# A list scheduler sets the order of all instructions, and matmuls on a zero tile fill TensorE's waits before the first feed-forward

## The chip, the cores and the metric

One core of a Trainium2 chip. The metric is the device time of one execution in microseconds (us), the median of the runs taken; a single core has no second core to compare its clock with, so a run is called slow only where it is over 1.5% above the fastest run of the same kernel. "Span" is the length of one profiled execution; it lies 1.7 us below the time of that same run.

## The reference, cut to what matters

```python
# r, k, v: [4, 8, 768, 48] (batch B, heads H, sequence S, head size D)
for t in range(S):                                    # linear attention with a decaying state
    cur = einsum('bhd,bhe->bhde', u * k_t, v_t)
    y[:, :, t] = einsum('bhd,bhde->bhe', r_t, state + cur)
    state = w * state + einsum('bhd,bhe->bhde', k_t, v_t)
x = y.transpose(0, 2, 1, 3).reshape(4, 768, 384)
X = fft(fft(x, axis=1), axis=2)                       # Fourier mixing
u = x + real(X)
un = (u - mean) / sqrt(var + 1e-6)                    # over the 384 columns
return u + relu(un @ w_ch1) @ w_ch2                   # 384 -> 1536 -> 384
```

Each batch passes through four stages: attention, the Fourier transform (two matmul steps), normalising, and the feed-forward. The Fourier transform of a batch needs all of its attention; the feed-forward of one half of a batch (384 rows) needs that half's normalised rows.

## The kernel before

The sequence is cut into 24 chunks of 128 rows, six to a batch. `phase1` multiplies k and r of a chunk by a decay table (VectorE, tile `KR`), turns the product with eight TensorE transposes (`tp`) and copies it to `KRT` (ScalarE). `phase2` makes the scores `A_ps`, masks them (`MA`) and updates the state; `phase3` makes the outputs `yd_ps` and `X`. After a batch's sixth chunk come the first Fourier step (matmuls from `XF`, copies `TT`), the second (matmuls from `TT` and its reversed copy `TR`, six additions `UF`), the statistics, and the normalised rows `UN`, which must be transposed (`UNT`) before the feed-forward. The order is that of a hand-written loop, which the framework's own scheduler refines; all loads and the DMA transposes of `UN` share the queue of SyncE and keep program order.

```python
    def phase1(i):
        ...
        nc.vector.tensor_tensor(out=KR..., in0=kr..., in1=wtab..., op=AluOp.mult)
        V = wp.tile([128, H, D], BF16, name="V", bufs=4)
        cv = nc.scalar.copy(V, vt)
        if i == 0:
            tc.keep_in_program_order(cv)
        tp = ps.tile([128, 2, NP, 128], BF16, name="tp", bufs=1)
        for s in range(2):
            for p in range(NP):
                nc.tensor.transpose(tp[:, s, p, :], KR[:, s, p, :], ident)
        KRT = wp.tile([128, 2, NP, 128], BF16, name="KRT", bufs=4)
        nc.scalar.copy(KRT, tp)
    ...
            sp(nc.sync.dma_start_transpose(out=UNT.rearrange("p j c t -> p (j c) t"),
                                           in_=UN.rearrange("p j d -> p (j d)")))
    ...
    INP = 6                                   # chunks of input held at once
    for i in range(INP):
        load(i)
    load_tables()
    FG = None                                 # the Fourier transform under way
    MSTART = 10
    for s in range(NC + 2):
        if s < NC:
            phase1(s)
        if INP <= s + INP - 2 < NC:
            load(s + INP - 2)
        if FG:
            FG = FG if advance(FG, 3 if s < 12 else 1) else None
        if s >= MSTART:
            feed(2)                           # up to two pieces of feed-forward work
        if 1 <= s < NC + 1:
            phase2(s - 1)
        ...
        if s >= 2:
            phase3(s - 2)
        ...
    feed(len(M))
```

Of the kernel before, what the change touches and what calls it, by code (L numbers as in the profile page):

```python
# [15 lines left out]
B = 4  # L16
# [44 lines left out]

@with_exitstack
def kernel(
# [31 lines left out]

    icol_i = cp.tile([128, 1], mybir.dt.int32, name="icol_i")
# [49 lines left out]
    def load_tables():  # L146
        sp(nc.sync.dma_start(out=te_t, in_=te_c.ap()))
        sp(nc.sync.dma_start(out=to_t, in_=to_c.ap()))
        sp(nc.sync.dma_start(out=hid_t, in_=hid_c.ap()))

    def load_w1():
        with tc.issue_after(marks[2].ins):
            for dt in range(3):
                nc.gpsimd.dma_start(out=W1[:, dt, :], in_=w1[dt * 128:(dt + 1) * 128, :])

    def load_w2():
        with tc.issue_after(marks[6].ins):
            for fg in range(3):
                nc.gpsimd.dma_start(out=W2[:, fg * 4:(fg + 1) * 4, :],
                                    in_=w2[fg * 512:(fg + 1) * 512, :].rearrange("(f p) d -> p f d", p=128))  # L160

    marks = {}

    def sp(ins):
        return tc.keep_in_program_order(ins)

    NC = B * NQ
    bat = [{} for _ in range(B)]
    chk = [{} for _ in range(NC)]

    def load(i):
        b, q = divmod(i, NQ)
        sl = slice(q * 128, (q + 1) * 128)
        kr = inp.tile([128, 2, H, D], F32, name="kr")
        vt = inp.tile([128, H, D], F32, name="vt")
        sp(nc.sync.dma_start(out=kr[:, 0], in_=k[b, :, sl, :].rearrange("h p d -> p h d")))  # L176
        sp(nc.sync.dma_start(out=kr[:, 1], in_=r[b, :, sl, :].rearrange("h p d -> p h d")))
        if i == 0:
            sp(nc.sync.dma_start(out=ident, in_=id_c.ap()))
        sp(nc.sync.dma_start(out=vt, in_=v[b, :, sl, :].rearrange("h p d -> p h d")))  # L180
        if i == 0:
            sp(nc.sync.dma_start(out=mtri, in_=mtri_c.ap()))
        chk[i]["in"] = (kr, vt)


    def phase1(i):
        c = chk[i]
        kr, vt = c["in"]
        KR = KRs[i % NB]
        nc.vector.tensor_tensor(  # L190
            out=KR.rearrange("t s p (a d) -> t (s p) a d", a=2)[:, :, :, 0:D],
            in0=kr.rearrange("t s (p a) d -> t (s p) a d", a=2),
            in1=wtab.rearrange("t s (p a d) -> t (s p) a d", a=2, d=D), op=AluOp.mult)
        V = wp.tile([128, H, D], BF16, name="V", bufs=4)
        cv = nc.scalar.copy(V, vt)  # L195
        if i == 0:
            tc.keep_in_program_order(cv)
        tp = ps.tile([128, 2, NP, 128], BF16, name="tp", bufs=1)
        for s in range(2):
            for p in range(NP):  # L200
                nc.tensor.transpose(tp[:, s, p, :], KR[:, s, p, :], ident)  # L201
        KRT = wp.tile([128, 2, NP, 128], BF16, name="KRT", bufs=4)
        nc.scalar.copy(KRT, tp)  # L203
        PR = wp.tile([128, NP, 128], BF16, name="PR", bufs=4)
        nc.vector.tensor_tensor(out=PR, in0=KRT[:, 0], in1=KRT[:, 1], op=AluOp.mult)  # L205
        c.update(KR=KR, V=V, KRT=KRT, PR=PR)

    def phase2(i):
        b, q = divmod(i, NQ)
        c = chk[i]  # L210
        KR, V, KRT = c["KR"], c["V"], c["KRT"]
        A_ps = [ps.tile([128, NP, 128], F32, name="A_ps", bufs=2) for _ in range(2)]
        for p in range(NP):
            for a in range(2):
                rows = slice(a * 64, a * 64 + 64)
                nc.tensor.matmul(A_ps[a][:, p, :], lhsT=KRT[rows, 0, p, :], rhs=KRT[rows, 1, p, :],  # L216
                                 start=(p == 0), stop=(p == NP - 1), skip_group_check=True)
        MAs = []
        for a in range(2):
            MA = wp.tile([128, NP, 128], BF16, name="MA", bufs=6)  # L220
            if a == 0 and b > 0:
                nc.vector.tensor_tensor(out=MA, in0=A_ps[a], in1=mtri.unsqueeze(1).to_broadcast([128, NP, 128]),
                                        op=AluOp.mult)
            else:
                AC = wp.tile([128, NP, 128], BF16, name="AC", bufs=2)
                nc.scalar.copy(AC, A_ps[a])  # L226
                nc.gpsimd.affine_select(out=MA, in_=AC, pattern=[[0, NP], [1, 128]], base=0,  # L227
                                        channel_multiplier=-1, compare_op=AluOp.is_gt, fill=0.0)
            MAs.append(MA)
        S = c.get("S")  # L230
        if q < NQ - 1:
            u_ps = ps.tile([128, NP, 2, D], F32, name="u_ps", bufs=1)
            for p in range(NP):
                nc.tensor.matmul(u_ps[:, p, :, :], lhsT=KR[:, 0, p, :], rhs=V[:, 2 * p:2 * p + 2, :],
                                 start=(p == 0), stop=(q == 0 and p == NP - 1), skip_group_check=True)
            if q > 0:
                nc.tensor.matmul(u_ps, lhsT=ident, rhs=S, start=False, stop=True, skip_group_check=True)
            Sn = wp.tile([128, NP, 2, D], BF16, name="Sst", bufs=4)
            nc.vector.tensor_tensor(out=Sn, in0=u_ps, in1=WD, op=AluOp.mult)
            chk[i + 1]["S"] = Sn  # L240
        c["MA"] = MAs

    def phase3(i):
        b, q = divmod(i, NQ)
        c = chk[i]
        V, KRT, PR, MAs, S = c["V"], c["KRT"], c["PR"], c["MA"], c.get("S")
        if q == 0:
            bat[b]["X"] = bp.tile([128, NQ, DM], BF16, name="X")
            bat[b]["EO"] = bp.tile([128, 2, 3, DM], BF16, name="EO", bufs=1)
            bat[b]["XF"] = bp.tile([128, 2, 3, DM], BF16, name="XF")  # L250
        X = bat[b]["X"]
        yd_ps = ps.tile([128, DM + H], F32, name="yd_ps", bufs=1)
        y_ps = yd_ps[:, 0:DM].rearrange("t (h d) -> t h d", h=H)
        for p in range(NP):
            nc.tensor.matmul(yd_ps[:, DM + 2 * p:DM + 2 * p + 2], lhsT=PR[:, p, :], rhs=UW[:, p, :],
                             start=(p == 0), stop=False, skip_group_check=True)
        if q > 0:
            for p in range(NP):
                nc.tensor.matmul(y_ps[:, 2 * p:2 * p + 2, :], lhsT=KRT[:, 1, p, :], rhs=S[:, p, :, :],
                                 start=False, stop=False, skip_group_check=True)  # L260
        DE = wp.tile([128, H], F32, name="DE")
        nc.scalar.copy(DE, yd_ps[:, DM:])  # L262
        TT = wp.tile([128, H, D], BF16, name="TT")
        marks[i] = nc.gpsimd.tensor_tensor(out=TT, in0=V, in1=DE.unsqueeze(2).to_broadcast([128, H, D]),  # L264
                                           op=AluOp.mult)
        for a in range(2):
            for p in range(NP):
                h = 2 * p + a
                nc.tensor.matmul(y_ps[:, h, :], lhsT=MAs[a][:, p, :], rhs=V[:, h, :],  # L269
                                 start=False, stop=(h == H - 1), skip_group_check=True)  # L270
        nc.vector.tensor_tensor(out=X[:, q, :], in0=yd_ps[:, 0:DM],  # L271
                                in1=TT.rearrange("p h d -> p (h d)"), op=AluOp.add)
        if b == 0 and q >= 3:
            fold(b, q - 3, q - 2)
        elif q == NQ - 1:
            fold(b, 0, 3)

    def fold(b, n0, n1):
        X, EO, XF = bat[b]["X"], bat[b]["EO"], bat[b]["XF"]
        lo, hi = X[:, n0:n1, :], X[:, n0 + 3:n1 + 3, :]  # L280
        nc.vector.tensor_tensor(out=EO[:, 0, n0:n1, :], in0=lo, in1=hi, op=AluOp.add)
        nc.vector.tensor_tensor(out=EO[:, 1, n0:n1, :], in0=lo, in1=hi, op=AluOp.subtract)
        e, o = EO[:, :, n0:n1, 0:192], EO[:, :, n0:n1, 192:384]
        nc.vector.tensor_tensor(out=XF[:, :, n0:n1, 0:192], in0=e, in1=o, op=AluOp.add)
        nc.vector.tensor_tensor(out=XF[:, :, n0:n1, 192:384], in0=e, in1=o, op=AluOp.subtract)


    def fourier(b):
        X, XF = bat[b]["X"], bat[b]["XF"]
        TT = bp.tile([128, 3, 2, 386], BF16, name="TT2")  # L290
        TR = bp.tile([128, 3, 2, 384], BF16, name="TR", bufs=1)
        for cb in range(3):
            for par in range(2):
# [163 lines left out]
```

## Time and profile before

| | before |
|---|---|
| time, median of 3 (lowest to highest) | 235.19 us (232.9 to 235.21) |
| span of the profile | 233.5 us |
| first feed-forward matmul starts | 63.7 us |
| from there to the end of the last matmul | 164.6 us |
| from there to the end of the span | 5.2 us |

The last three rows add up to the span (63.7 + 164.6 + 5.2 = 233.5). The first is a stretch in which loads, VectorE, ScalarE and TensorE hand work to one another and no engine is full. The second is a stretch in which TensorE has all of the feed-forward to do; what it takes above the warm duration of that work is idle time and half clock. The prediction below shows the lines.

### The profile page before, as it was taken

The page shows a single profiled execution, that of the slowest core. Times are in us where ns is not written, and L with a number is a line of the kernel's source. Part 1 is how long each engine was busy: PE and PEld are TensorE (multiplying, and loading weights), DVE is VectorE, ACT ScalarE, POOL GpSimd, SP SyncE. Part 2 cuts the span into 40 slices and gives each one's busy share as a digit, 9 for nine tenths or more (in the row PEclk, how much of TensorE's full clock was granted, in tenths as well). Part 3 has the DMA queues.
Part 4 walks back from the last instruction along what each step waited for, and adds up shares of the span by engine and source line. Part 5 has one row for each costly group of instructions (what it writes and reads, how often), then busy time and mean ns, then how long its engine had stood idle before and what let it go on. Part 6 is the DMA issues. An engine that isn't in the chain of part 4 may idle for free.

```text
span 233.5 us, 4269 instructions
## 1 busy us (share of the span) xinstructions
PE 191.2 (82%) x1640; PEld 122.3 (52%) x1640; DVE 131.1 (56%) x273; ACT 129.3 (55%) x261; POOL 64.1 (27%) x93
## 2 busy tenths in 40 slices
PE   0289856991798979987999789964999999999990
PEld 0156634670555645665565456652565565566660
DVE  4367479795955694598881454782841277101020
ACT  4677534734798675577247564543356637654500
POOL 4038944701213441343100133162001000101021
PEclk9999999999599988995599999995699999999998
DMA  5999999999999996101603940102003103310111
GB/s 108 187 188 197 284 206 186 181 190 190 175 177 166 208 182 137 36 0 36 121 34 66 210 70 10 36 34 53 0 34 84 36 34 86 84 70 35 67 70 67
DMA packets 88917, 25.33 MB, mean 108 GB/s; under 512 B 85312, under 2 KB 86976, under 8 KB 88896
## 3 DMA queue, kind: packets, MB, share of 16 engines
q1 hardware_dynamic: 85216, 17.96, 44.7%
q0 software_dynamic: 3680, 7.08, 11.8%
q8 instruction: 13, 0.21, 0.4%
q14 instruction: 8, 0.07, 0.1%
HBM read 20.32 MB, written 4.72 MB: 107 GB/s over the span
## 4 chain that ended last, share of the span: by engine, by line
issue 29%; PE 22%; ACT 11%; DMA 11%; POOL 9%; DVE 8%; SPq 6%; POOLq 0%; ACTq 0%; DVEq 0%
PE mm L353 6%; PE mm L362 5%; DMA vt<-in_v_dram 5%; DMA kr<-in_r_dram 5%; POOL TT L264 4%; POOL out_dram L367 3%; ACT KRT L203 3%; PE tp L201 3%; ACT HT L355 2%; ACT UN L337 2%; POOL MA L227 2%; SPq L176 2%; PE mm L298 2%; PE A_ps L216 2%; DMA UNT<-UN 2%
## 5 line engine op out<-in xcount | busy, mean ns | idle before, releaser
L355 ACT ACTIVATE HT<-mm 128x384 bf16<-128x384 f32 x96 | 46.0, 497 | 35.1 <-PE mm L353 34.7
L353 PE MATMUL mm<-UNT,W 128*128 128x384 bf16 x288 | 59.2, 341 | 2.7 <-DMA UNT<-UN 1.7
L362 PE MATMUL mm<-W,HT 128*128 128x384 bf16 x288 | 51.4, 331 | 0.0
L353 PEld LDWEIGHTS <-W 128*128 128x128 bf16 x288 | 28.3, 101 | 21.2 <-issue 4.8
L362 PEld LDWEIGHTS <-HT 128*128 128x128 bf16 x288 | 28.6, 99 | 19.5 <-issue 1.6
L365 DVE TENSOR_TENSOR osb<-mm,UF 128x384 f32<-128x384 f32 x24 | 13.4, 557 | 43.2 <-PE mm L362 43.1
L367 POOL DMA_DIRECT2D out_dram<-osb x24 | 13.3, 555 | 87.9 <-DVE osb L365 87.9
L227 POOL TENSOR_SCALAR_AFFINE_SELECT MA<-AC 128x512 bf16<-128x512 bf16 x30 | 22.2, 751 | 40.1 <-ACT AC L226 35.5
L264 POOL TENSOR_TENSOR TT<-V,DE 128x384 bf16<-128x384 bf16 x24 | 22.6, 941 | 36.4 <-ACT DE L262 34.2
L190 DVE TENSOR_TENSOR KR<-kr,wtab 128x768 bf16<-128x768 f32 x24 | 23.7, 991 | 12.9 <-DMA kr<-in_r_dram 12.9
L201 PE MATMUL tp<-ident,KR 128*128 128x128 bf16 x192 | 20.0, 258 | 12.3 <-DVE KR L190 11.5
L203 ACT COPY KRT<-tp 128x1024 bf16<-128x1024 bf16 x24 | 24.3, 1012 | 7.7 <-PE tp L201 7.3
L201 PEld LDWEIGHTS <-KR 128*128 128x128 bf16 x192 | 15.0, 116 | 15.4 <-DVE KR L190 13.4
L216 PE MATMUL A_ps<-KRT 64*128 64x128 bf16 x192 | 15.4, 257 | 9.0 <-ACT KRT L203 4.4
L226 ACT CAST AC<-A_ps 128x512 bf16<-128x512 f32 x30 | 17.2, 592 | 9.9 <-PE A_ps L216 9.8
L271 DVE TENSOR_TENSOR X<-yd_ps,TT 128x384 bf16<-128x384 f32 x24 | 13.3, 553 | 14.8 <-POOL TT L264 14.4
L195 ACT CAST V<-vt 128x384 bf16<-128x384 f32 x24 | 12.4, 515 | 12.6 <-POOL TT L264 6.6
L300 ACT CAST TT<-mm 128x386 bf16<-128x386 f32 (+1 forms) x24 | 14.1, 603 | 5.6 <-PE mm L298 5.5
L337 ACT ACTIVATE UN<-UF,nm,rstd 128x384 bf16<-128x384 f32 x24 | 15.2, 697 | 3.6 <-DVE nm L333 3.5
L216 PEld LDWEIGHTS <-KRT 64*128 64x128 bf16 x192 | 8.5, 108 | 15.5 <-issue 7.4
L205 DVE TENSOR_TENSOR PR<-KRT 128x512 bf16<-128x512 bf16 x24 | 11.3, 471 | 8.5 <-ACT KRT L203 8.4
L269 PE MATMUL yd_ps<-V,MA 128*128 128x48 bf16 x192 | 11.0, 199 | 5.3 <-ACT DE L262 3.5
(64 smaller groups left out, 239.7 us busy)
## 6 DMA issues: line engine op xcount, KB each, us to landing
kr<-in_k_dram SPq DMA_DIRECT2D x24, 192.0 KB, 4.6
kr<-in_r_dram SPq DMA_DIRECT2D x24, 192.0 KB, 4.6
vt<-in_v_dram SPq DMA_DIRECT2D x24, 192.0 KB, 4.7
out_dram<-osb POOLq DMA_DIRECT2D x24, 192.0 KB, 2.2
W<-in_moe_w_ch_dram POOLq DMA_DIRECT2D x6, 384.0 KB, 7.6
hid_t<-hid_c SPq DMA_DIRECT2D x1, 576.0 KB, 5.7
te_t<-te_c SPq DMA_DIRECT2D x1, 289.5 KB, 4.8
to_t<-to_c SPq DMA_DIRECT2D x1, 288.0 KB, 4.5
```

The costliest lines, as they stand in the source:

```text
L190: nc.vector.tensor_tensor(out=KR.rearrange("t s p (a d) -> t (s p) a d", a=2)[:, :, :, 0:D], in0=kr.rearrange("t s (p a) d -> t (s p) a d" ...
L201: nc.tensor.transpose(tp[:, s, p, :], KR[:, s, p, :], ident)
L203: nc.scalar.copy(KRT, tp)
L216: nc.tensor.matmul(A_ps[a][:, p, :], lhsT=KRT[rows, 0, p, :], rhs=KRT[rows, 1, p, :], start=(p == 0), stop=(p == NP - 1), skip_group_check ...
L226: nc.scalar.copy(AC, A_ps[a])
L227: nc.gpsimd.affine_select(out=MA, in_=AC, pattern=[[0, NP], [1, 128]], base=0, channel_multiplier=-1, compare_op=AluOp.is_gt, fill=0.0)
L264: marks[i] = nc.gpsimd.tensor_tensor(out=TT, in0=V, in1=DE.unsqueeze(2).to_broadcast([128, H, D]), op=AluOp.mult)
L337: nc.scalar.activation(out=UN[:, j, :], in_=UF[:, j, :], func=Act.Identity, scale=rstd[:, j:j + 1], bias=nm[:, j:j + 1])
L353: nc.tensor.matmul(hp, lhsT=W1[:, dt, ft * 128:(ft + 1) * 128], rhs=UNT[:, :, dt, :], start=(dt == 0), stop=(dt == 2))
L355: nc.scalar.activation(out=HTs[hf][:, ft, :], in_=hp, func=Act.Relu)
L362: nc.tensor.matmul(op, lhsT=HTs[hf][:, ft, j * 128:(j + 1) * 128], rhs=W2[:, ft, :], start=(ft == 0), stop=(ft == 11))
L367: nc.gpsimd.dma_start(out=out[b, row:row + 128, :], in_=osb)
```

## The change

The intent is to keep TensorE busy, and so at full clock, from the start, and to begin the feed-forward earlier. In the profile of the kernel before, the granted clock was 1.00 at 46 to 53 us, where TensorE was busy for 6.98 of 7 us, and 0.58 at 60 to 66 us, after a stretch with 1.36 busy us of 7. Every operation is entered with its engine, a duration, what it reads and what it writes; a list scheduler plays these through and writes out the order, which the framework's scheduler is told to leave alone. Zero matmuls are offered to TensorE at the lowest priority until 46 us of the scheduler's clock. Beside this, batch 0's `UN` is turned by TensorE transposes in place of the DMA transpose, loads are held in 4 buffers and not 6, and the second feed-forward matmul is split in halves. The diff, cut to its core:

```diff
+class _Schedule:
+    LATENCY = 80
+    LANDING = 1900
+    COLD = 8000
+    ...
+    def order(self):
+        ...
+            for e, ops in cand.items():
+                at = free.get(e, 0.0)
+                pick = None
+                ops[:] = [o for o in ops if o["until"] is None or at < o["until"]]
+                for o in ops:
+                    t = room(o)               # when a buffer is free
+                    if t is None:
+                        continue
+                    start = max(at, o["ready"], t + self.LATENCY)
+                    key = (start, o["pri"], o["n"])
+                    if pick is None or key < pick[0]:
+                        pick = (key, o)
+                if pick and (best is None or pick[0] < best[0]):
+                    best = pick
+        ...
+    def emit(self):
+        for o in self.order():
+            ...
+            o["fn"]()
...
-        kr = inp.tile([128, 2, H, D], F32, name="kr")          # pool of 6
+        c["kr"] = kr = new(inp, [128, 2, H, D], F32, "kr", 4)
+        op("SP", 600, lambda: nc.sync.dma_start(out=kr()[:, 0], in_=...),
+           w=[("k", i)], new=[kr], dma=1030, pri=10 * i - 50)
...
-        cv = nc.scalar.copy(V, vt)
-        if i == 0:
-            tc.keep_in_program_order(cv)
+        op("ACT", 510, lambda: nc.scalar.copy(V(), vt()), r=[("v", i), "wtab"], w=[("V", i)], new=[V], use=[vt], pri=pri + 1)
...
+            if b == 0:
+                for j in range(3):
+                    turned(sh, j, UN, UNT)    # 3 transposes into PSUM, one VectorE copy
+                ...
+                return
+            op("SP", 1200, lambda: nc.sync.dma_start_transpose(...), ...)
...
+    def idle():
+        z = new(ps, [128, 512], F32, "mm", 3)
+        op("PE", 216, lambda: nc.tensor.matmul(z(), lhsT=zero[:, 0:128], rhs=zero, start=True, stop=True),
+           r=["zero"], w=[("idle", len(sch.ops))], new=[z], pri=10 ** 6, until=WARM)
+    WARM = 46000
+    for _ in range(220):
+        idle()
...
-    for s in range(NC + 2):                   # the loop shown above
-        ...
-    feed(len(M))
+    with tc.manual_schedule():
+        sch.emit()
```

## The prediction

> **What bounds the kernel now.** I read the page first (busy shares, slices), then busy time by stretch, then TensorE's timeline for the clock at which matmuls ran, then the queue of the loads, and the chain of waits last.

> ```profile
> span 233.5 us, 4269 instructions
> PE 191.2 (82%) x1640; PEld 122.3 (52%) x1640; DVE 131.1 (56%) x273; ACT 129.3 (55%) x261; POOL 64.1 (27%) x93
> PE   0289856991798979987999789964999999999990
> DMA  5999999999999996101603940102003103310111
> ```

> TensorE is the bound on average, but not from the start: until about 90 us the DMA engines are full, TensorE only from about 65 us, and it has holes near 55, 105 and 155 us. Its 191.2 us are no fixed quantity either:

> ```profile
> 18.01 1.03 PE L201 MATMUL tp<-ident,KR 128*128 128x128 bf16 x8 [0.28 <-DVE KR L190]
> ...
> 41.28 1.03 PE L201 MATMUL tp<-ident,KR 128*128 128x128 bf16 x8
> 45.76 0.62 PE L201 MATMUL tp<-ident,KR 128*128 128x128 bf16 x8
> ...
> 60.88 1.03 PE L201 MATMUL tp<-ident,KR 128*128 128x128 bf16 x8
> ...
> 66.79 0.61 PE L201 MATMUL tp<-ident,KR 128*128 128x128 bf16 x8
> ```

> The reader is to see the same eight transposes at 1.03 us and at 0.61: until 45.8 us TensorE runs at half rate, and again around 60. The table by stretch shows the rest (PEclk reads 1.00 before 46 us only because no clock event was recorded yet):

> ```profile
> core 0: us, PE busy (x) PEld busy (x) DVE busy (x) ACT busy (x) POOL busy (x), PEclk, DMA share, GB/s
> 46.00:53.00 7.00, 6.98 (x87) 5.24 (x84) 6.71 (x18) 3.00 (x7) 1.24 (x3) 1.00 1.27 191
> 53.00:60.00 7.00, 1.36 (x17) 0.94 (x16) 4.47 (x15) 4.00 (x8) 0.38 (x1) 0.87 1.01 190
> 60.00:66.00 6.00, 5.42 (x49) 3.44 (x47) 5.55 (x11) 4.47 (x10) 1.42 (x2) 0.58 0.86 152
> 100.00:110.00 10.00, 7.97 (x112) 5.99 (x109) 9.21 (x22) 7.09 (x16) 4.65 (x7) 0.80 0.01 2
> 110.00:115.00 5.00, 4.55 (x38) 3.07 (x38) 4.15 (x7) 1.68 (x4) 1.26 (x2) 0.50 0.96 177
> 150.00:160.00 10.00, 6.15 (x94) 4.59 (x92) 6.28 (x15) 4.81 (x11) 3.80 (x6) 0.86 0.05 20
> 160.00:170.00 10.00, 8.38 (x56) 5.02 (x53) 6.29 (x12) 2.13 (x5) 1.44 (x2) 0.63 0.16 31
> ```

> Each hole is followed by a stretch at half clock. Attention for the last chunks ends only near 163 us. Loads are issued in program order with the DMA transposes between them, so the queue stands still for tens of us:

> ```profile
> SPq L339 <- ACT HT L355: 55.3, 5, 18.8
> ...
> SPq L339 <- ACT DE L262: 28.9, 2, 26.3
> ```

> The first feed-forward matmul starts at 63.7 us although the first Fourier transform's matmuls end at 52: ScalarE stands behind a load (its cast of vt waits until 55.04), so the statistics wait for it.

> [...] The trace agrees on the two rates ((1.03-0.22)/7 = 116 ns per transpose against (0.61-0.22)/7 = 56 ns). [...] the drops near 105 and 158 us come with TensorE still partly busy, and 28.8 us busy of the 38 between 8 and 46 us did not wake it. So a filler must make it dense, not just present. [...] 216 ns for the 512-column fillers, an estimate; the trace has 163 ns at 384 columns, which fits. [...]

> **The change part by part.**

> 1. *Fillers.* The instruction order of the changed kernel holds 73 zero matmuls: 15 ahead of the first transposes, 58 between there and the first feed-forward, mostly six per chunk. The 15 lie in start-up, where TensorE has nothing until 8.1 us: free[...]. The 58 x 0.216 = 12.5 us lie in slots that were waits. With loads paced at about 3.1 us a chunk (three issues of about 1.0 us), TensorE has 1.5 us of warm attention work and 6 x 0.216 = 1.3 us of filler, 2.8 of 3.1: dense enough to stay warm. Direct gain: shorter links of the chain to the first feed-forward (transposes 1.03 to 0.61, scores 0.61 to 0.40).

> 2. *Order.* The first feed-forward now comes after 9 chunks' transposes instead of after 11, batch 0's normalised tile is turned by 18 TensorE transposes (18 x 0.058 = 1.0 us of TensorE, six copies of about 0.45 us on VectorE) instead of a DMA transpose with 3.4 us to landing, and loads no longer stand behind the later DMA transposes until chunk 22.

> 3. *TensorE's work, all warm.* From start-to-start times in warm stretches: feed-forward 576 x 0.163 = 93.9; first Fourier step 72 x 0.163 = 11.7; second 24 groups x (2 x 0.163 + 4 x 0.083) = 15.8; attention: transposes 24 x 0.47 = 11.3, scores 24 x 0.33 = 7.9, state 20 x 0.18 + 16 x 0.165 = 6.2, outputs 24 x (0.11 + 0.24) + 20 x 0.165 = 11.7; the new transposes 1.0. Sum 159.5 us, against 191.2 counted now, the difference being mostly half rate.

> 4. *When the first feed-forward starts.* Chunk 8 must be turned before it in the new order. In the kernel before its multiply ran at 44.75, behind the same tables and first weights, at the same full DMA. Normalising, turning and copying end at about the same time. I put the start at 47 us, 16.7 earlier. By then 20.3 of the 159.5 us are done (counting the new order up to there); 139.2 remain.

> 5. *From there to the last attention output.* TensorE has 67.8 us of work up to the last chunk's transposes, some 70 to its outputs. VectorE, counted in the new order at its back-to-back rates (KR 0.88, the 384-column operations 0.47, mask 0.60, Fourier folds 0.68), has 70.6 us in the same stretch; ScalarE some 64. Three engines so nearly level do not all stay full: I allow 10 us of TensorE idle. Loads should not be the limit: chunk 17's data at about 45 + 9 x 3.1 + 6.5 (the second weights: two issues in the queue took 4.57 and 3.93 us in place of about 1.0 each) = 79 us, wanted at 47 + 35 = 82. Stretch end 47 + 70 + 10 = 127.

> 6. *From there on.* 139.2 - 70 = 69 us, nearly all feed-forward, which ran at 163 ns a matmul without gaps after 170 us in the kernel before: 196, with 1 us for the last Fourier transform 197. One half-clock episode costs 2 to 5 us; I take half of a 4 us one: 199. But part of the 10 us of idle is the same waiting as such an episode, so I subtract 2: 197.

> 7. *Tail.* Unchanged: from the last matmul (228.3) to the end (233.5) 5.2 us. Span 202.2. The timed figure lies 1.7 us above the span (235.19 against 233.5): 204. Steps 5 and 6 lean to caution on an order made with durations close to those measured (feed-forward triple 495 ns, transposes 460), so I take 202 us.

> The saving of 33 us splits as follows: half clock and idle ahead of the first feed-forward 16.7; after it, TensorE needed 164.6 us (63.7 to 228.3) for some 137 us of warm work, 28 lost, and I expect 11 to 13 lost instead.

> **The rivals.**

> *A: the fillers do not wake the clock.* Then six at 0.43 us plus 3.0 us of cold attention come to 5.6 us a chunk against 3.1 us of loads, and the fillers stand in program order ahead of real work: the first feed-forward moves to 55 or 60 and the end to 210 to 216. For it: transposes and mostly waiting matmuls did not wake the clock before 45.8 us. Against: the long burst at the start, and the dense stretch at 41 to 45.7 us that did wake it.

> *B: VectorE becomes the bound between 47 and 127 us.* It is at 9.21 of 10 us between 100 and 110 us already, with TensorE dropping to half clock just then. No fillers exist after the first feed-forward. If idle is 20 us instead of 10 with two clock drops, the end is 214 to 218. Against: the new order puts feed-forward work into such holes.

> *C: loads stay the limit and only the order of waiting changes.* The DMA engines are full until 90 us and the bytes are the same; with 4 input buffers instead of 6 the queue may stall where a buffer is released late. Then chunks 12 to 17 come late and the time is 208 to 212. The stalls of the queue for DMA transposes speak against more than this.

> *D: everything packs.* No clock drop after the first feed-forward and 4 us of idle: 192 to 194.

> **Range and chances.** D marks the lower side, A and B the upper: 190 to 214 should hold it 8 times in 10, with 202 between. For a gain under 2% (above 230.5) both A and B would have to come fully and more: 0.04 within 2%, 0.02 slower, 0.94 faster.

> **What would show it.** Step 1: the first eight transposes take about 0.61 us in all, and no half-rate stretch lies before 47 us. Step 4: the first feed-forward matmul near 47 us. Step 3: TensorE's busy time near 175 us (159.5, 16 of fillers, a little half rate). Step 5: last attention output near 127 us, VectorE above 85% busy between. Step 6: the last 30 us or more solid feed-forward. It would be wrong if the transposes still take 1.03 us before 45 us, if the fillers sit ahead of work that was already ready, or if TensorE idles over 20 us after the first feed-forward.

## The result, and the profile after

The changed kernel takes 210.28 us (median of 4 runs, 208.91 to 211.41), the kernel before in the same rounds 234.46 us (232.9 to 235.21). The ratio is 0.8974, with a 95% interval of 0.8893 to 0.9054. All ratios here are the mean time of one kernel's fast runs over that of the other's fast runs of the same rounds, so they are not quite the ratios of the medians quoted.

| | before | after | difference | predicted |
|---|---|---|---|---|
| first feed-forward matmul | 63.7 | 56.8 | -6.9 | 47 |
| from there to the last matmul's end | 164.6 | 147.6 | -17.0 | 150 |
| tail | 5.2 | 5.3 | +0.1 | 5.2 |
| span | 233.5 | 209.7 | -23.8 | 202.2 |

The span is shorter by 23.8 us, and 17.0 of these lie after the first feed-forward matmul. There TensorE was idle for 13.7 us before (164.6 less 150.95 busy) and for 5.2 us now (147.6 less 142.40), and its clock stood at half for some 25 us before and for 3.4 now. (The profiled run of the changed kernel, at 211.41 us, was the slowest of its four.) The page of the changed kernel, first its busy shares, then TensorE's busy tenths and its clock in 40 slices:

```profile
PE 186.7 (89%) x1729; PEld 118.7 (57%) x1731; DVE 136.0 (65%) x281; ACT 129.5 (62%) x260; POOL 64.0 (31%) x92
PE   7199975599999699999789999999999999999990
PEclk9969998569999999999969999999999999999999
```

A slice is 5.24 us here. The reader is to see that the holes of the kernel before are gone from TensorE's row, except for a 6 at 68 to 73 us and a 7 and an 8 at 100 to 110, and that the row is all but full from there to the end. Yet TensorE's row dips between 26 and 42 us and the clock's between 31 and 47, in the stretch that was to be warm, and the clock dips once more in the third slice.

TensorE's timeline up to the first feed-forward shows that dip (columns: start, us, engine, line, operation, tiles, count; in brackets the idle time ahead and who ended it):

```profile
1.26 4.96 PE L614 MATMUL mm<-zero 128*128 128x512 bf16 x15 [1.26 <-DVE wuc L233]
10.77 0.62 PE L327 MATMUL tp<-ident,KR 128*128 128x128 bf16 x8 [4.54 <-DVE KR L317]
...
35.84 1.04 PE L327 MATMUL tp<-ident,KR 128*128 128x128 bf16 x8 [1.11 <-DVE KR L317]
...
50.57 0.62 PE L327 MATMUL tp<-ident,KR 128*128 128x128 bf16 x8
...
56.78 1.14 PE L582 MATMUL mm<-UNT,W 128*128 128x384 bf16 x6
```

The fifteen fillers at the start did wake the clock: the clock record reads full from 4.45 us, and the first eight transposes take 0.62 us, not 1.03. They also start later than in the kernel before (10.77 against 8.11 us), since ScalarE now has its first cast of `vt`, which waits for a load until 8.18 us, ahead of the exponentials that make the decay table. From 35.8 to about 45 us the matmuls run at half rate all the same, and for some us after 11 too (five fillers took 2.33 us there, 1.24 at 25.3).

By stretches of 10 us, after the first feed-forward (columns as in the prediction):

```profile
60.00:70.00 10.00, 10.00 (x124) 6.88 (x123) 8.57 (x14) 8.88 (x21) 6.82 (x8) 1.00 1.03 158
...
100.00:110.00 10.00, 7.91 (x76) 4.73 (x75) 9.29 (x23) 6.63 (x13) 3.82 (x6) 0.84 0.61 133
...
150.00:160.00 10.00, 10.00 (x74) 6.67 (x73) 5.09 (x12) 4.99 (x10) 0.96 (x2) 1.00 0.11 39
```

At 150 to 160 us, where the kernel before had 6.15 us of 10 busy, TensorE is full. The one bad stretch is 100 to 110 us, with VectorE at 9.29: TensorE waits there twice, and then runs at half clock for three us.

```profile
104.73 0.38 PE L341 MATMUL A_ps<-KRT 64*128 64x128 bf16 x7 [1.37 <-DVE MA L348]
...
107.48 2.10 PE L582 MATMUL mm<-UNT,W 128*128 128x384 bf16 x6
```

Six feed-forward matmuls take 2.10 us where the line at 56.78 shows 1.14.

Now the miss, the start at 56.8 and not 47 us. The chain of waits, in order of time (start, us, what):

```profile
30.78 8.97 DMA vt<-in_v_dram
39.87 0.38 issue
40.24 0.58 ACT AC L353
40.82 0.50 ACT TT L470
41.37 0.80 PE mm L463 x2
42.25 0.34 PE yd_ps L411 x8
42.59 2.25 PE mm L463 x7
```

Chunk 7's `vt` took 9 us to arrive, its issue alone 4.12 us in the queue in place of about 1.0, just after the three loads of the first weights (27.45 to 29.14 us; the issue of chunk 6's `vt` at 24.67 us had already taken 3.00). ScalarE's cast of it stands in order ahead of the Fourier copies (`TT`), and three matmul results wait for those copies: TensorE stood for 1.70 us ahead of 41.37, and the first Fourier step ended at 44.8 us. What then still lies ahead of the first feed-forward is on VectorE's timeline:

```profile
47.07 0.56 DVE L508 TENSOR_TENSOR UF<-mm,X 128x384 f32<-128x384 f32 x1 [0.26 <-PE mm L502]
...
48.01 2.89 DVE L508 TENSOR_TENSOR UF<-mm,X 128x384 f32<-128x384 f32 x5
50.82 0.55 DVE L513 BATCH_NORM_STATS2 st<-UF 128x6 f32<-128x384 f32 x1
...
53.48 0.16 DVE L528 SCALAR_TENSOR_TENSOR nm<-MV,rstd 128x3 f32<-128x3 f32 x1
...
56.12 0.61 DVE L557 COPY UNT<-mm 128x384 bf16<-128x384 bf16 x2
```

The second step's additions end at 50.9 us, the statistics of the first half at 53.6, and normalising (ScalarE, 53.68 to 55.58), turning and copying end at 56.7. The first feed-forward matmul follows 0.05 us later. From the end of the first Fourier step that is 12 us (56.8 - 44.8). Part of the gain on the kernel before is in the last link: from the last normalised row of that half to the feed-forward it took 4.2 us there (59.52 to 63.73), by the DMA transpose, and takes 1.2 here (55.58 to 56.78), by TensorE and VectorE (a VectorE copy of a turned tile took 0.35 to 0.36 us; the prediction put about 0.45). Of the 6.9 us by which the feed-forward starts earlier, 3.0 lie in this link.

The loads show once more, later. SyncE's queue issued loads to 56.75 us, then waited for a free `kr` buffer until 59.98 (VectorE read one until 59.95, with chunk 9's multiply); the second weights were issued from 62.33 us on. Chunk 14 then arrived late, on VectorE's timeline and on TensorE's:

```profile
71.70 0.96 DVE L317 TENSOR_TENSOR KR<-kr,wtab 128x768 bf16<-128x768 f32 x1 [2.55 <-DMA kr<-in_r_dram]
```

```profile
73.17 0.24 PE L391 MATMUL yd_ps<-UW,PR 128*128 128x2 bf16 x4 [2.07 <-DVE X L415]
```

### The profile page after: what moved, and what is told of

Same layout as the page of the kernel before. It is cut to its first block, busy times and chain, and to the rows that moved or that the text cites. A ratio compares the mean times of both kernels' runs of the same rounds, so it can differ in the third digit from the quotient of the medians.

```text
span 209.7 us, 4438 instructions
## 1 busy us (share of the span) xinstructions
PE 186.7 (89%) x1729; PEld 118.7 (57%) x1731; DVE 136.0 (65%) x281; ACT 129.5 (62%) x260; POOL 64.0 (31%) x92
## 4 chain that ended last, share of the span: by engine, by line
PE 37%; issue 27%; DVE 11%; DMA 11%; POOL 6%; ACT 3%; SPq 2%; POOLq 0%; ACTq 0%; DVEq 0%
PE mm L598 7%; DMA vt<-in_v_dram 6%; PE mm L582 5%; DMA kr<-in_r_dram 5%; PE mm L614 4%; PE tp L327 4%; POOL out_dram L608 4%; PE mm L463 3%; DVE KR L317 3%; PE mm L498 3%; PE A_ps L341 2%; PE u_ps L369 2%; DVE XF L439 2%; DVE X L415 1%; PE yd_ps L411 1%
## 5 line engine op out<-in xcount | busy, mean ns | idle before, releaser
L582 PE MATMUL mm<-UNT,W 128*128 128x384 bf16 x288 | 53.7, 330 | 0.5 <-DVE osb L605 0.3
L355 POOL TENSOR_SCALAR_AFFINE_SELECT MA<-AC 128x512 bf16<-128x512 bf16 x29 | 19.4, 676 | 50.4 <-ACT AC L353 49.3
L402 POOL TENSOR_TENSOR TT<-V,DE 128x384 bf16<-128x384 bf16 x24 | 25.0, 1040 | 27.7 <-ACT DE L401 27.0
L608 POOL DMA_DIRECT2D out_dram<-osb x24 | 13.3, 554 | 62.6 <-DVE osb L605 57.6
L353 ACT CAST AC<-A_ps 128x512 bf16<-128x512 f32 x29 | 16.6, 591 | 11.7 <-PE A_ps L341 11.7
L614 PE MATMUL mm<-zero 128*128 128x512 bf16 x71 | 20.1, 423 | 1.4 <-DVE wuc L233 1.3
L327 PE MATMUL tp<-ident,KR 128*128 128x128 bf16 x192 | 15.7, 229 | 5.8 <-DVE KR L317 5.6
L327 PEld LDWEIGHTS <-KR 128*128 128x128 bf16 x192 | 12.4, 103 | 9.1 <-DVE KR L317 6.4
L470 ACT CAST TT<-mm 128x386 bf16<-128x386 f32 (+1 forms) x24 | 12.7, 600 | 4.3 <-PE mm L463 4.3
L331 DVE TENSOR_TENSOR PR<-KRT 128x512 bf16<-128x512 bf16 x24 | 14.1, 596 | 0.5 <-ACT KRT L330 0.4
L508 DVE TENSOR_TENSOR UF<-mm,X 128x384 f32<-128x384 f32 x24 | 12.7, 551 | 1.8 <-PE mm L502 1.1
L348 DVE TENSOR_TENSOR MA<-A_ps,mtri 128x512 bf16<-128x512 f32 x19 | 12.9, 681 | 1.1 <-PE A_ps L341 1.0
```

The source lines that it names most:

```text
L327: nc.tensor.transpose(tp()[:, s, p, :], KR()[:, s, p, :], ident)
L353: op("ACT", 590, lambda: nc.scalar.copy(AC(), A_ps[a]()), r=[("A", i)], w=[("AC", i, a)], new=[AC], use=[A_ps[a]], pri=pri)
L355: op("POOL", 680, lambda: nc.gpsimd.affine_select(out=MA[a](), in_=AC(), pattern=[[0, NP], [1, 128]], base=0, channel_multiplier=-1, compa ...
L402: op("POOL", 850, lambda: nc.gpsimd.tensor_tensor(out=TT(), in0=V(), in1=DE().unsqueeze(2).to_broadcast([128, H, D]), op=AluOp.mult), r=[( ...
L582: nc.tensor.matmul(hp(), lhsT=W1[:, dt, ft * 128:(ft + 1) * 128], rhs=UNT()[:, :, dt, :], start=(dt == 0), stop=(dt == 2))
L608: op("POOL", 550, lambda: nc.gpsimd.dma_start(out=out[b, row:row + 128, :], in_=osb()), r=[("osb", hf, j)], w=[("out", hf, j)], use=[osb], ...
```

## The experiments

The questions were three. Does the order or do the fillers carry the 24 us? Which link of the chain ahead of the first feed-forward makes it 56.8 and not 47 us? And what would a version without those links take? All times are medians beside the kernel before on the same chip in the same rounds (its medians were 234.13 to 235.21 us). Where some runs of a kernel were slow, the median is that of its fast runs. "Start of the feed-forward" is read from the one profile of each run; in the versions of the changed kernel it varied between 54.9 and 58.5 us, and by 1.7 us between two versions whose order is the same (56.78 in the changed kernel, 58.47 with six buffers), so a difference of that size in it shows little by itself.

### The new order without the fillers

```diff
-        for o in self.order():
+        for o in (o for o in self.order() if o["until"] is None):
```

> The scheduler's order kept instruction for instruction, only the 73 zero matmuls left out. Theory (the order carries most of the gain; up to the first feed-forward VectorE, the loads and ScalarE set the pace, and TensorE only adds its links to the chain): TensorE runs at half rate until about 45 us, each chunk's links grow by about 0.6 us, the first feed-forward matmul moves from 56.8 to 59 to 61 us and the time from 210 to 212 to 215 us. Rival (the fillers carry the gain): the first feed-forward moves to 65 us or more, near the 63.7 us of the kernel before, and the time is over 220 us. Third: the fillers cost as much as they give, time within 1 us of 210.

Measured: 211.51 us (210.58 to 211.84), ratio 0.9015 (0.8953 to 0.9076). The interval overlaps that of the changed kernel: by the means the fillers are worth about 1 us, and that is not told apart from nothing. The start of the feed-forward:

```profile
10.66 1.03 PE L327 MATMUL tp<-ident,KR 128*128 128x128 bf16 x8 [10.66 <-DVE KR L317]
...
20.27 0.62 PE L327 MATMUL tp<-ident,KR 128*128 128x128 bf16 x8
...
56.95 1.95 PE L582 MATMUL mm<-UNT,W 128*128 128x384 bf16 x6
```

The first transposes run at half rate, but from 19.6 us on the order alone has woken the clock, which in the kernel before first rose at 44.5 us. It does not last: by the trace's clock records it is at half again from 29.8 to 46.9 us, and from 57.1 to 60.5. The feed-forward starts at the same time as with fillers, its first six matmuls at half rate. TensorE's busy time falls from 186.7 to 174.5 us with 1 us of time at stake: those 12 us were work in waits that nothing else needed.

### The fillers on the kernel before

```diff
+    fill(15)                                  # 15 zero matmuls, then 3 + 3 a chunk for ten chunks
     for s in range(NC + 2):
         ...
+        if s < MSTART:
+            fill(3)
         if 1 <= s < NC + 1:
             phase2(s - 1)
+        if s < MSTART:
+            fill(3)
```

> The kernel before with fillers alone: 15 zero matmuls at the start and six per chunk for the first ten chunks, its own order otherwise. Theory (order carries most): the transposes take 0.61 us in place of 1.03 for most of the first 45 us, but the first feed-forward still waits for the tenth chunk by program order, so it starts within 2 us of 63.7 and the time is 231 to 236 us, ratio 0.985 to 1.005. Rival (fillers carry the gain): 215 to 225 us, ratio under 0.96.

Measured: 234.12 us, ratio 0.9969 (0.9887 to 1.005): the same.

```profile
7.92 0.62 PE L203 MATMUL tp<-ident,KR 128*128 128x128 bf16 x8 [0.58 <-DVE KR L192]
...
64.60 4.28 PE L355 MATMUL mm<-UNT,W 128*128 128x384 bf16 x15 [0.62 <-DMA UNT<-UN]
```

The transposes are at full rate from the start (of those up to 46 us only the ones at 40.73 us are not), and the feed-forward starts at 64.60 us (63.7 before). VectorE's multiply ahead of the second chunk's transposes still waits 2.56 us for its load (2.62 before). Together the two runs settle the first question: the order carries the gain, and not the fillers. "The order" here includes the edits that came with it; of these the buffers were tested apart (below), the turning of batch 0 by TensorE, the halved matmul and the later loads of the second weights were not.

### ScalarE's first cast behind the decay table's exponentials

```diff
-   nc.scalar.copy(V(), vt())
+   (tc.keep_in_program_order if i == 0 else (lambda x: x))(nc.scalar.copy(V(), vt()))
```

> The changed kernel with ScalarE's first cast of vt pinned behind the exponentials that make the decay table, as in the kernel before; no other instruction is moved. Theory (the lateness of the first feed-forward, 56.8 against 47 forecast, adds up from 3.4 us at the start, 3 us of slowed VectorE and a wait for a load at 39.8 us that is independent of both): the first multiply by the table moves from 9.75 to about 7.1 us, but the cast of chunk 7 still waits for its load until about 39 us, so the first feed-forward gains 0 to 1.5 us and the time is 208.5 to 210.5. Rival (the start shifts everything behind it): the first feed-forward at 53.5 and the time 207.

Measured: 208.85 us (208.11 to 209.32 in the three fast runs; a fourth, the profiled one, was slow at 212.46), ratio 0.8893 (0.883 to 0.8957). The feed-forward starts at 56.93 us. So the 2.7 us that the start lost at the first cast do not reach the feed-forward: the loads pace the chunks that follow. The ratio is lower than the changed kernel's, but the intervals overlap.

### Chunk 7's cast behind the first Fourier copies

```diff
-        for o in self.order():
+        for o in _moved(self.order()):
...
+    behind(("V", 7), ("TT2", 0, 2, 0))        # the cast goes after that copy in the order
```

> The changed kernel with one instruction moved: ScalarE's cast of chunk 7's vt goes behind five of the six copies of the first Fourier step, which stood behind it while its load was late (it landed at 39.8 us). Theory: the copies start when their matmuls end (about 38.5 us), the first feed-forward starts 1 to 2 us earlier than 56.8, the time falls to 208 to 209.5. Rival (the copies wait for TensorE at half clock, not for the cast): no change, 210. Moved together with the start of the other run the gains would add up.

Measured: 208.91 us (the three fast runs 208.3 to 210.14; a fourth, the profiled one, was slow at 215.06), ratio 0.8908 (0.8839 to 0.8977). This slow profile has the feed-forward's start at 55.21 us and this:

```profile
74.28 0.24 PE L391 MATMUL yd_ps<-UW,PR 128*128 128x2 bf16 x4 [4.74 <-DVE X L415]
```

The hole of 2.07 us has grown to 4.74: the same loads are waited for, only for longer. As it is a slow run, this shows where the time can go, not how much a fast run loses there.

### Without GpSimd's product (wrong result)

Between 20 and 40 us VectorE was busy for 9.70 and 9.28 us of each 10. Part of that is `PR`, the product of two tiles in SBUF: it took 0.86 to 1.05 us for chunks 1 to 4, with GpSimd's product running beside it, and 0.41 us where no GpSimd instruction ran. Here GpSimd's product `TT` is left out and `X` adds zeros.

```diff
-        op("POOL", 850, lambda: nc.gpsimd.tensor_tensor(out=TT(), in0=V(), in1=DE()..., op=AluOp.mult),
+        op("POOL", 850, lambda: None,
...
-            out=X()[:, q, :], in0=yd()[:, 0:DM], in1=TT()..., op=AluOp.add),
+            out=X()[:, q, :], in0=yd()[:, 0:DM], in1=zero[:, 0:384], op=AluOp.add),
```

> Wrong result on purpose: GpSimd's product TT is left out and VectorE adds a tile of zeros in its place; all else in the same order. Theory (VectorE is slowed before 47 us by sharing with GpSimd: the product PR took 0.93 to 1.05 us there in place of 0.41, the multiply by the table up to 1.6 in place of 0.95): PR takes 0.41 us for chunks 1 to 4, the fold of chunk 5 ends 2 to 3 us earlier than 38.0 us, but the cast of chunk 7 still waits for its load until about 39.8, so the first feed-forward gains under 1.5 us; the time falls to 207 to 210. Rival (VectorE is what makes the first feed-forward late): first feed-forward at 54 or earlier and 206 us or less.

Measured: 210.25 us, ratio 0.8968 (0.8888 to 0.9048), on three fast runs of five; the start of the feed-forward at 57.55 us in a slow profile, with chunk 7's cast at 39.80 us as before (39.83). `PR` took 0.41 to 0.43 us for every chunk up to 60 us, so its slowing beside GpSimd is real (the multiply by the table still took up to 1.39; GpSimd's masking stayed in this run), but it is not what sets the time.

### A third of the first weights loaded (wrong result)

```diff
-  lhsT=W1[:, dt, ft * 128:(ft + 1) * 128]
+  lhsT=W1[:, 0, ft * 128:(ft + 1) * 128]      # and two of the three loads left out
```

> Wrong result on purpose: of the first feed-forward weights only a third is loaded and used three times; all else in the same order. Theory (the 768 KB of the other two thirds run beside the loads of chunks 6 and 7, and ScalarE stands in order behind the cast of chunk 7): that cast runs at 35 to 37 us in place of 39.8, the first feed-forward at 53.5 to 55 in place of 56.8, the time 206.5 to 208.5. Rival (the loads are late for another reason): the cast within 1 us of 39.8 and the time 210.

Measured: two of four runs were slow, the fast ones took 209.68 and 211.38 us, ratio 0.8983 (0.8895 to 0.907). In the (slow) profile chunk 7's cast came at 38.57 us and the feed-forward at 55.08; the hole at 72.76 us was 3.36 us long. The first weights cost about 1 us at the cast, far less than the 10 us sought, and even that did not shorten the whole.

### The first half's statistics before the second half's additions

VectorE makes all six additions `UF` before the first half's statistics. Here the second half's three additions and statistics go behind the first half's, and the 16 fillers that lie there are left out.

```diff
+    for j in (5, 4, 3):
+        behind(("UF", 0, j), ("nm", 0, 0))
+    ...
+    first, last = todo.index(at["u", 8]), todo.index(at["tq", 0, 0])
+    todo = [o for n, o in enumerate(todo) if o["until"] is None or not first < n < last]
```

> Valid result. VectorE's six residual additions of batch 0 no longer all run ahead of the first statistics: the second half's three, and its statistics, stand behind the first half's scale, and the 16 fillers ahead of the first turned tile are left out, since they would wait for those additions. Theory (from the end of the first Fourier transform on, the first feed-forward waits for VectorE's order): it starts at 54.5 to 55.5 us in place of 56.8 and the time is 208 to 209.5. Rival (what is gained there is lost after it, since the loads then set the pace up to 75 us): first feed-forward earlier, time still 210. If the clock drops in the idle gap that the fillers leave, the first feed-forward runs at half rate and the gain is lost too.

Measured: 212.75 us (211.76 to 214.58), ratio 0.9087 (0.9016 to 0.9157). The feed-forward started at 57.47 us, and its first six matmuls took 1.83 us. The gain that was expected did not come. Chunk 7's cast was at 40.61 us in this profile, 0.8 us later than in the changed kernel's, and TensorE then idled for 2.82 us ahead of the turning, with the clock down after it. As two things changed at once, the order and the 16 fillers, the run does not tell which made it slower (by its mean; the interval meets the changed kernel's).

### The three moves together

```diff
+  (tc.keep_in_program_order if i == 0 else (lambda x: x))(nc.scalar.copy(V(), vt()))
+  behind(("V", 7), ("TT2", 0, 2, 0))
+  ...                                       # and the edit just above, whole
```

> Valid result: the three moves together (first cast behind the tables, cast of chunk 7 behind the Fourier copies, first half first). Theory (the delays are in one chain, so the gains add up once the cast of chunk 7 is out of the way): first feed-forward at 50.5 to 52.5 us, time 204 to 206.5. Rival (the loads bound the stretch up to 75 us): first feed-forward at 52, time 208 or more.

Measured: 210.11 us (209.76 to 210.25), ratio 0.8963 (0.8912 to 0.9013), with the first cast, chunk 7's cast and the first-half order all moved. The feed-forward started at 56.05 us with its first six matmuls at half rate (1.96 us), and the hole at 71 to 73 us was gone. The gains that were expected of the single moves did not add up.

### Six input buffers, same order

```diff
-                    t.value = pool.tile(shape, dtype, name=name, bufs=t.bufs)
+                    t.value = pool.tile(shape, dtype, name=name, bufs=6 if name in ("kr", "vt") else t.bufs)
```

> Valid result. The input buffers kr and vt are six deep again, as in the kernel before, in place of four; the order of every engine and queue is kept, only the loads' waits for a free buffer become shorter. Theory (what sets the time up to about 75 us is the arrival of chunk 14's k and r, wanted at 71.6 us: the load queue stood from 56.8 to 60.0 us for a free buffer, with the DMA engines 0.37 busy, and then met the second weights): those loads are issued 2 to 3 us earlier, TensorE's 2.1 us hole before 73.2 us closes, the time falls by 1.5 to 2.5 us to 207.5 to 209. Rival (the DMA engines have no spare time ahead of it, so earlier issue only queues): the hole stays at 71 to 73 and the time is 210.

Measured, in five rounds: 210.32 us (209.26 to 212.13), ratio 0.8995 (0.8949 to 0.9042). The queue of loads, on its own timeline:

```profile
52.38 2.94 SPq L301 DMA_DIRECT2D vt<-in_v_dram  x3
55.41 0.91 SPq L295 DMA_DIRECT2D kr<-in_k_dram  x1
```

It no longer stands: the load that waited until 59.98 us is issued at 55.41, and TensorE has no hole at 71 to 73 us. The time did not move. In this profile the half clock before the feed-forward lasted from 34.5 to 48.1 us and the feed-forward started at 58.47, which is 1.7 us later; that the hole's 2 us were lost there is read from this one profile, and not shown.

### A third of the second weights loaded (wrong result)

```diff
-   rhs=W2[:, ft, :]
+   rhs=W2[:, ft % 4, :]                       # and two of the three loads left out
```

> Wrong result on purpose: a third of the second weights is loaded and used three times; same order otherwise. Theory (the second weights, issued at 62.3 us, delay chunk 14's loads): the hole of 2.1 us at 71.1 to 73.2 us goes, the first feed-forward stays at 56.8, the time falls by 1.5 to 2.5 us. Rival (bound elsewhere after 75 us): hole gone, time within 0.5 us of 210.

Measured, in five rounds: 209.52 us (208.29 to 211.4), ratio 0.8947 (0.8905 to 0.8989). The hole is gone here too, and the time is within 0.8 us of the changed kernel's. So by the means the loads between 57 and 75 us are not worth more than a us.

### Six buffers and the two moved casts

The edit of the six buffers, that of the first cast and that of chunk 7's cast; the half-order move is left out, since it had brought nothing.

```diff
+  bufs=6 if name in ("kr", "vt") else t.bufs                                 # six buffers
+  (tc.keep_in_program_order if i == 0 else (lambda x: x))(nc.scalar.copy(V(), vt()))
+  behind(("V", 7), ("TT2", 0, 2, 0))
```

> Valid result. Six input buffers, the first cast behind the tables and the cast of chunk 7 behind the Fourier copies, the fillers all kept. Theory (an earlier first feed-forward is worth nothing by itself because chunk 14's loads then make the wait, as the hole of 4.7 us in the run with the cast of chunk 7 moved showed; with the loads earlier it counts): first feed-forward at 55 us or earlier, hole under 2 us, time 206 to 208, the fastest so far. Rival (the loads stay the bound at 71 us however issued): 209 to 210.

Measured, in five rounds: 208.35 us (207.42 to 208.84), ratio 0.8897 (0.8864 to 0.8929), in the same rounds as the 0.8995 of six buffers alone: the two casts are worth about 1% once the buffers are there. (Moving the first cast alone gave 0.8893 with 4 buffers, and chunk 7's alone 0.8908. So which of the two it is stays open, and so does whether the buffers are needed for it.) There was no hole at 71 to 73 us and no half clock after the feed-forward began (from 56.81 us), though TensorE's wait of 1.37 us was there, at 101 to 103 us, and the one of 0.63 us after it.

### The same without the fillers

```diff
-        for o in _moved(self.order()):
+        for o in (o for o in _moved(self.order()) if o["until"] is None):
```

> The version with six buffers and the two moved casts, in the same order, without the zero matmuls. If the fillers carry nothing (what the run of the changed kernel without them left open, as its interval overlapped): 208 to 209.5 us, ratio within 0.005 of 0.890, first feed-forward matmul 56 to 58 us. If they are worth something once the loads and casts are out of the way (a full clock from 47 us on in the profile with them): a half-clock stretch before or just after the first feed-forward matmul, and 210.5 to 213 us, ratio 0.898 or more. The first transposes take about 1.0 us for eight either way.

Measured, in five rounds: 208.18 us (207.4 to 208.95), ratio 0.8857 (0.8825 to 0.889). The fillers are worth nothing that shows here. The half clock of the expectation's second case is there, on TensorE's timeline, and costs nothing that counts:

```profile
8.00 1.03 PE L327 MATMUL tp<-ident,KR 128*128 128x128 bf16 x8 [8.00 <-DVE KR L317]
...
54.92 2.10 PE L582 MATMUL mm<-UNT,W 128*128 128x384 bf16 x6
```

The first six feed-forward matmuls run at half rate, but they start earlier in this profile than in any other. This is the fastest version measured, simpler than the changed kernel, and correct: about 1% faster than it (the intervals 0.8825 to 0.889 and 0.8893 to 0.9054 just fail to meet). It is also the best of nine correct versions, picked after the fact, and its median differs by only 0.17 us from that of the version with fillers (208.18 and 208.35).

## Why the prediction was right, and where its size was off

The direction, the class and the range (190 to 214 us) held; the time was 8 us longer than the 202 of the prediction. The mechanism was the order, as predicted, in two parts: an earlier feed-forward and a much denser stretch after it. The third part, the direct gain of the fillers, did not come.

**Step 4 failed.** It put the first feed-forward matmul at 47 us. Half of its anchor was good: chunk 8's multiply ran at 42.12 us, before the 44.75 us of the kernel before. But its transposes, which were to come before the feed-forward, stood behind the second Fourier step and ran at 50.57 us (45.76 before). What failed further is the sentence that follows: "Normalising, turning and copying end at about the same time." They ended 14.6 us after the start of that multiply (56.7 - 42.1), because the Fourier transform of batch 0 was not finished when chunk 8 was multiplied. The first step ended at 44.8 us, and 12 us of second step, six additions, statistics, normalising, turning and copying still followed, one after another. This chain was never added up in the prediction, though nearly all its parts were in the profile before. The term is 9.8 us too small (56.8 - 47), and it is more than the whole miss: 204 + 9.8, less 2.4 for the stretch after it (147.6 measured, 150 predicted), is 211.4, which is the time of the profiled run. The 2 us taken off at the end, for an order that was made with durations close to those measured, had no ground.

The runs show no single link ahead of this chain that holds those 10 us. A third of the first weights, the chunk 7 cast, the first cast, GpSimd's product and the half order were each taken up alone, and the start stayed between 55.1 and 57.6 us (four of these five profiles are slow runs). Nor did any run shorten the chain itself: in all twelve traces of the changed kernel and its versions the first Fourier step ends between 43.3 and 45.5 us and the feed-forward starts 11.0 to 12.9 us later. What the chain's beginning would be with ideal loads was not tried.

**Step 1 was half right.** The fifteen fillers wake the clock: 0.62 us for the first eight transposes. But "no half-rate stretch lies before 47 us" was wrong: there was one from 11.3 to 14.7 us and one from 35.2 to 45.4, the second while TensorE waited for loads and the ScalarE copies. And the direct gain given to them, shorter links to the first feed-forward, is not there: the two runs without fillers and the one with fillers alone show by their means at most about 1 us. The size of a filler was right (16 of them took 3.62 us, 0.38 for one alone: 216 ns from one to the next at full clock, and 427 ns at half, between 1.66 and 4.22 us; 163 ns at 384 columns, scaled to 512, gives 217). The prediction's 116 ns for a transpose at half clock was not: it took off the 0.22 us that a single one takes at full clock; eight in a row against three at half clock, (1.03 - 0.50)/5, give 106.

**Step 3.** TensorE's busy time is 186.7 us, not 175. Without fillers it is 174.5, so the fillers made 12 us of it, where the prediction put 16. The term that was too small is "a little half rate": 174.5 is 15 us above the 159.5 us of warm work.

**Step 5 was off where it did no harm.** The last attention outputs came at 145.5 us, not at 127. Of this 9.8 us is step 4's. The last chunk's transposes ran at 132.3 us, 75.5 us after the feed-forward began, against 67.8 us of work: within the 10 us of idle that were allowed. But its outputs came another 13 us later, where the prediction had 2, since the order puts feed-forward matmuls between; these are work that had to be done anyway. From the first feed-forward to these outputs VectorE was busy for 74.5 us of 88.7, 84%, where above 85% was predicted.

**Steps 6 and 7 held.** Some 139.2 us of warm work took 147.6 us: 8.4 us lost, 11 to 13 predicted. There was one half-clock episode, of 3.41 us by the clock records; at half rate that costs some 1.7 us, an estimate. (In the kernel before the three between 65 and 228 us took 3.41, 10.24 and 10.24 us: 1.7 to 5.1 us each by the same estimate, where the prediction put 2 to 5.) From 145.5 us to the end of the last matmul TensorE was busy for 58.6 us of 58.9, and the tail is 5.3 us.

**The rivals.** *A* did not come, though its figures (a start at 55 to 60 us, an end at 210 to 216) hold what was measured, by chance: the fillers do wake the clock, and a start at 56.8 us has other causes, as it is the same without them. *B* came in small: VectorE full from 104 to 110 us, two waits of 2.0 us in sum and a drop of the clock. The drop is worth some 1.7 us, an estimate (half rate for 3.41 us). The version with six buffers and moved casts has the same two waits and no drop, and so has the one without fillers. The traces point to where the waits fall. The changes of the clock lie on a fixed grid of 3.41 us (last section), and in the changed kernel nearly all of both waits fell into one interval of it, after which the clock dropped (columns as in the prediction; TensorE's busy time comes second):

```profile
103.43:106.84 3.41, 1.52 (x29) 1.10 (x29) 3.38 (x10) 2.48 (x5) 0.80 (x2) 1.00 0.75 183
```

With six buffers and moved casts an edge of the grid lay between them, and the clock stayed up:

```profile
100.38:103.79 3.41, 1.95 (x26) 1.06 (x24) 3.14 (x10) 1.94 (x4) 0.92 (x2) 1.00 0.77 187
103.79:107.20 3.41, 2.78 (x46) 1.90 (x44) 3.41 (x7) 2.49 (x7) 2.20 (x3) 1.00 0.57 113
```

A busy time near 2 us goes both ways in the traces of the kernel before and the changed kernel: full-clock windows with 1.73, 1.78, 1.81 and 2.26 us kept the clock, and others with 1.70, 2.03 and 2.38 us lost it. So this drop and its absence were in good part luck. *C* came in part: the queue stood for 3.2 us for a free buffer and there was a hole of 2.07 us, but six buffers closed it for no gain in time. That the 210.28 us lie in *C*'s 208 to 212 is therefore chance too. *D* did not come.

## What to carry to other kernels

Before moving a milestone in an estimate, add up the chain of dependent operations from the last input to it; a sum of engine work says when a stage can end, never when it can begin. Filler matmuls must be switched off, in a run of their own, before they get the credit for a gain: here they woke the clock, and the time was the same. Where several delays lie side by side ahead of one milestone, try them together before calling any of them harmless: six buffers, two moved casts and no fillers together gave 1%, while none of these alone could be told from the changed kernel. That it takes all of them is not shown: the first cast alone measured 0.8893, in a wider interval.
